# Attention and two MLPs on one core: three changes of order, and one operation of chunk 0 moved from VectorE to ScalarE

## The chip, the core and the metric

The kernel runs on one core of a Trainium2 chip. The metric is the device time of one execution in microseconds; the number to predict is the median over several executions of the changed kernel.

## What is computed

Four batches of 576 tokens go through an attention of eight heads of 64 (four heads look at the last 32 positions, four at every 32nd), then through two MLPs of 512 to 2048 to 512 features, all 2304 tokens. The weights come as float64.

```python
x = attention(q, k, v)                      # 2304 x 512
h = x @ w_in;   g = h * clip(h + 3, 0, 6) / 6;             x = g @ w_out
h = x @ w_in2;  g = maximum(h, 0) + log1p(exp(-abs(h)));   out = g @ w_out2
```

## The kernel before

Every large product is made of three matmuls, with each operand split into a high part (a rounding of 32 bits to the matmul's format) and a low part (the rest): high x high, high x low, low x high. ScalarE makes the high part with a copy, VectorE the low part with a subtraction. The float64 weights are loaded as raw 64-bit words; `w_scale` (L132, ScalarE) rescales the upper words and `w_bits` (L137 and L140, VectorE) puts three bits of the lower words under them, which gives float32 weights.

The **first MLP** is a row of 80 slots, 16 (one for each block f of 128 hidden features) for each of five chunks of tokens: chunk 0 of 384 tokens, the others of 480. `slot` (L1289) emits the hidden matmuls of its own f (`pe_h`, L776: psh from x and W_in), the activation (`post1`, `post2a`, `post2b`: L789, L790, L797, L803), and the output matmuls of the slot two before (`pe_y`, L820: psy from gh, gl and the halves woh, wol of W_out). Each is 12 matmuls. In chunk 0 a slot also makes the weights: `win_bits` and `win_split` for W_in, `wout_bits` and `wout_split` (L170 to L176) for W_out. Pieces of the attention for the next chunk are strewn between them from the table `fill`. From the eighth slot of chunk 1 on, two parts per slot of `prep` turn the weights of the second MLP into sums of blocks and their halves (L230, L248, L249), stored to the DRAM tiles sdr and sorted by a counter `k0` (L1293).

The **second MLP** uses Strassen's scheme, seven products in place of eight. Three chunks of 768 tokens (order `CHS`: 1, 2, 0) each have a first phase (`pe1`, L933, banks psm: 8 groups g of 7 units i) and a second one (`pe2`, L1077, banks psa and psn: 7 products of 8 units). A unit is six matmuls of 384 columns. `steps` (L1354) is the order of all units. A unit's weights su are loaded 10 units ahead on SP's queue (L908), and after each such load SP issues one waiting transfer of the list `dmas`: the stores of the output and the loads of the next chunk's x (`x_load`, xr from ydr), in the order in which `queue` (L883) took them. The loaded x pieces are summed on VectorE by `x_sums` (L859) in the same first phase. In that phase product 7 and then product 4 of a group add into one bank, and between them VectorE reads it (u, L915).

On each engine the instructions of a slot or unit keep the order in which they are written (`in_order`), so an instruction that waits holds all behind it. `do` (L1373) ties the casts and subtractions of the second phase's input (th, tl: L1008, L1012) to units.

Of the kernel before, what the change touches and what calls it, by code (L numbers as in the profile page):

```python
# [13 lines left out]
ALU = mybir.AluOpType  # L14
# [8 lines left out]
def attn_two_mlps(  # L23
# [21 lines left out]
    nc = tc.nc  # L45
# [6 lines left out]
    NF = DFF // P  # L52
# [15 lines left out]
    HT, NF2, DH = 384, NF // 2, DM // 2  # L68
# [55 lines left out]
    def words(o, l, f, dt):  # L124

        w = wst_t[o, l, f].bitcast(dt).rearrange("p (n t) -> p n t", t=2)
        return w[:, :, 0], w[:, :, 1]

    def w_scale(o, l, f):

        h = words(o, l, f, U32)[1].bitcast(F32)
        nc.scalar.activation(out=h, in_=h, func=AF.Prelu, scale=2.0**-112, alpha=-(2.0**32))  # L132

    def w_bits(o, l, f, out=None):
        low, _ = words(o, l, f, U32)
        m, e = words(o, l, f, I32)
        nc.vector.tensor_scalar(  # L137
            out=m, in0=low, scalar1=2.0**-29, scalar2=7.0, op0=ALU.mult, op1=ALU.min
        )
        nc.vector.scalar_tensor_tensor(  # L140
            out=e if out is None else out.bitcast(I32), in0=e, scalar=3, in1=m,
            op0=ALU.logical_shift_left, op1=ALU.bitwise_or,
        )
# [6 lines left out]
    def win_bits(f):  # L150
        wi_t[0, f] = sw_tile("wir", F32)
        w_bits(0, 0, f, wi_t[0, f])
        wst_t.pop((0, 0, f))
# [47 lines left out]
    def prep_load(o, g):  # L201
        for f in (2 * g, 2 * g + 1):
            (load_wout if o else load_win)(1, f)
# [633 lines left out]
    def half(c, t):  # L837

        return 2 * c + (t if c else 1 - t)

    def x_load(c, kl):
        raw = l2p["r" if kl and "r" in l2p else "x"].tile([P, 5, HT], F32, tag="xr", name="xr", bufs=1)
        xr_t[c, kl] = raw
        parts = []
        for slot, kt, t in ((0, kl, 0), (3, kl, 1), (1, kl + 2, 0), (2, kl + 2, 1)):
            a0 = a = half(c, t) * HT
            while a < a0 + HT:
                s = max(i for i in range(NC1) if Y0[i] <= a)
                z = min(a0 + HT, Y0[s + 1])
                parts.append((raw[:, slot, a - a0 : z - a0], ydr[s][kt, :, a - Y0[s] : z - Y0[s]]))  # L850
                a = z
        return parts
# [22 lines left out]
    pre, aft, dmas, now = {}, {}, [], [0]  # L875
# [4 lines left out]
    def after_post(d, fn, *a):  # L880
        aft.setdefault(now[0] + d, []).append(lambda: fn(*a))

    def queue(d, parts):  # L883
        dmas.extend((now[0] + d, o, i) for o, i in parts)

    @contextmanager
    def in_order():
# [105 lines left out]
    ORDER2 = (1, 5, 6, 2, 7, 4, 3)  # L993
# [134 lines left out]
    for b in range(B):  # L1128
        o = 2 * NF * b
# [33 lines left out]
    with ExitStack():  # L1163
# [5 lines left out]
        for i, t in enumerate(sq0):  # L1169
            nc.sync.dma_start(  # L1170
                out=t.rearrange("p (h i) d -> p h (i d)", h=2),
# [16 lines left out]
            out=mask, in_=mask, compare_op=ALU.is_ge, fill=NEG / SCALE, base=STRIDE,  # L1188
# [3 lines left out]
            out=ident, in_=ident, compare_op=ALU.not_equal, fill=1.0, base=0,  # L1192
# [3 lines left out]
            out=mask, in_=mask, compare_op=ALU.is_ge, fill=NEG / SCALE, base=-1,  # L1196
# [92 lines left out]
        def slot(n, l, c, f):  # L1289
            att = c < B  # L1290
            first_use = c == 0
            last1 = c == NC1 - 1
            k0 = 2 * n - 2 * NF - 14  # L1293

            if n == NF + 1:
                prep_load(0, 0)
            if last1 and f == 0:
                at.close()
                l2p["x"] = ctx.enter_context(tc.tile_pool(name="l2x", bufs=1, reuse_waits="tile"))
            pe_h(l, c, f)  # L1300
            if first_use:
                if f + 3 < NF:
                    w_scale(0, 0, f + 3)
                    win_bits(f + 3)
                if f + 2 < NF:
                    win_split(f + 2)
            post1(l, c, f)
            if not first_use:
                post2a(l, c, f)
            if att:  # L1310
                for u in fill.get(2 * n, []):
                    u()
            if first_use:
                w_scale(1, 0, f)
                wout_bits(f)
                post2a(l, c, f)
            post2b(l, c, f)
            if 0 < n <= NF:
                wout_split(n - 1)
            prep(k0)  # L1320
            if n >= 2:
                pe_y(*seq[n - 2])
            if att:
                for u in fill.get(2 * n + 1, []):
                    u()
            prep(k0 + 1)
            if first_use:
                load_first(2 * f + 11)
                load_first(2 * f + 12)
            if c == 1:  # L1330
                split_raw(c, f)
            if NF <= n + 3 < 2 * NF:
                load_raw(*seq[n + 3][1:])
            if 2 * NF <= n + 4 < len(seq):
                load_split(*seq[n + 4][1:])
            if last1 and f >= 1:
                kl, r = divmod(f - 1, 7)
                if r == 0 and kl < 2:
                    for o, i in x_load(CHS[0], kl):
                        nc.sync.dma_start(out=o, in_=i)  # L1340
                elif r == 3:
                    x_split(CHS[0], kl, 0)
                    x_sums(CHS[0], kl, False)
                elif r == 4:
                    x_sums(CHS[0], kl, True)
                    x_split(CHS[0], kl, 2)
                elif r == 5:
                    x_split(CHS[0], kl, 1)
# [5 lines left out]
        steps = []  # L1354
        for c in CHS:
            for g in range(NF2 + 1):
                for i in (1, -4, 6, -3, 2, 7, 5):
                    if (g < NF2) if i > 0 else (g > 0):
                        steps.append((c, 1, g - (i < 0), abs(i)))
            for i in ORDER2:  # L1360
                steps += [(c, 2, g, i) for g in range(NF2)]
        AHEAD = 10
        for k in range(AHEAD):
            s_unit(steps[k])
# [10 lines left out]

        for n, c in enumerate(CHS):
            nxt = CHS[n + 1] if n + 1 < NCH else None
            for k, gc, gs in ((3, 0, 1), (4, 1, 2), (5, 3, 4), (6, 4, 5), (7, 6, 7)):
                do(c, 1, gc, t_cast, c, k)
                do(c, 1, gs, t_sub, c, k)  # L1380
            for k in range(8, 4 * len(ORDER2)):
                p, q = divmod(k - 4, 4)
                do(c, ORDER2[p], 2 * q, t_cast, c, k)
                do(c, ORDER2[p], 2 * q + 1, t_sub, c, k)
            for i, g, j, q in (
                (5, 7, 7, 0), (6, 1, 7, 1), (6, 3, 7, 2), (2, 1, 7, 3),
                (2, 3, 4, 0), (2, 5, 4, 1), (7, 1, 4, 2), (7, 3, 4, 3),
            ):
                do(c, i, g, t_diff, c, j, q)
            if nxt is not None:  # L1390
                for i, g, kl, part in (
                    (5, 2, 0, 0), (5, 4, 1, 0), (3, 1, 0, 2), (3, 3, 1, 2), (3, 5, 0, 1), (3, 6, 1, 1)
                ):
                    do(c, i, g, x_split, nxt, kl, part)
                for kl in range(2):
                    do(c, 6, 5 + 2 * kl, x_sums, nxt, kl, True)
        for k, step in enumerate(steps):
            c, ph, g, i = step
            nxt = CHS[CHS.index(c) + 1] if c != CHS[-1] else None
            now[0] = k  # L1400
            with in_order():
                if k + AHEAD < len(steps):
                    s_unit(steps[k + AHEAD])
                for _ in range(1 if k + AHEAD < len(steps) else 2):
                    if dmas and dmas[0][0] <= k:
                        _, o, v = dmas.pop(0)
                        nc.sync.dma_start(out=o, in_=v)
                post = (pe1 if ph == 1 else pe2)(step)
                for u in pre.pop(k, []):
                    u()  # L1410
                early = ph == 1 and i == 3 and g in (2, 4, 6)
                if early:
                    t_cast(c, g // 2 - 1)
                if post:
                    post()
                if early:
                    t_sub(c, g // 2 - 1)
                for u in aft.pop(k, []):
                    u()
                if ph == 1:  # L1420
                    if nxt is not None and g in (1, 2) and i == 1:
                        queue(1, x_load(nxt, g - 1))
                    if nxt is not None and i == 2 and g in (4, 6):
                        x_sums(nxt, g // 2 - 2, False)
                else:
                    for u in at.get((c, i, g), []):
                        u()
# [70 lines left out]
```

## Time and profile before

| | us |
|---|---|
| three runs, median (lowest, highest) | 852.42 (848.24, 852.48) |
| profiled execution, its own time | 854.5 |
| its span | 852.6 |
| TensorE busy in it | 821.2 (96%) |
| VectorE busy | 636.0 (75%) |
| ScalarE busy | 456.9 (54%) |

In the profile, PE is TensorE's matmuls, PEld its weight loads, DVE VectorE, ACT ScalarE, POOL GpSimd, SP the engine that only issues transfers. A busy PE is the sum of modelled matmul intervals, which overlap; where it is busy throughout, the distance from start to start tells the pace. PEclk is the granted clock as a share of 2.4 GHz.

### The profile page before, as it was taken

The page shows a single profiled execution, that of the slowest core. Times are in us where ns is not written, and L with a number is a line of the kernel's source. Part 1 is how long each engine was busy: PE and PEld are TensorE (multiplying, and loading weights), DVE is VectorE, ACT ScalarE, POOL GpSimd, SP SyncE. Part 2 cuts the span into 40 slices and gives each one's busy share as a digit, 9 for nine tenths or more (in the row PEclk, how much of TensorE's full clock was granted, in tenths as well). Part 3 has the DMA queues.
Part 4 walks back from the last instruction along what each step waited for, and adds up shares of the span by engine and source line. Part 5 has one row for each costly group of instructions (what it writes and reads, how often), then busy time and mean ns, then how long its engine had stood idle before and what let it go on. Part 6 is the DMA issues. An engine that isn't in the chain of part 4 may idle for free.

```text
span 852.6 us, 16751 instructions
## 1 busy us (share of the span) xinstructions
PE 821.2 (96%) x6245; PEld 757.7 (89%) x6245; DVE 636.0 (75%) x1055; ACT 456.9 (54%) x754; POOL 88.5 (10%) x149
## 2 busy tenths in 40 slices
PE   5889999999999999999999999999998999999996
PEld 3779998888888888888888899999998999999996
DVE  5899966777776677866777568798667898587784
ACT  4567653455444444545555467854376834478530
POOL 3001122123211121111211200000000000000000
PEclk8899999999999999999999999999999999999998
DMA  9899777599969997796977798788899887997774
GB/s 308 227 281 328 160 232 269 143 342 343 373 206 244 302 334 281 217 302 201 328 269 259 247 359 258 243 250 245 259 281 311 247 246 220 303 306 245 247 248 114
DMA packets 169504, 225.42 MB, mean 264 GB/s; under 512 B 76432, under 2 KB 91664, under 8 KB 169424
## 3 DMA queue, kind: packets, MB, share of 16 engines
q1 hardware_dynamic: 154304, 176.71, 68.3%
q0 software_dynamic: 13312, 46.67, 14.5%
q10 hardware_dynamic: 1808, 0.98, 0.5%
q8 instruction: 50, 0.82, 0.4%
q14 instruction: 30, 0.25, 0.1%
HBM read 172.88 MB, written 51.38 MB: 263 GB/s over the span
## 4 chain that ended last, share of the span: by engine, by line
PE 56%; issue 17%; DVE 6%; ACT 4%; POOL 3%; DMA 3%; POOLq 0%; DVEq 0%; ACTq 0%; SPq 0%
PE psn L1077 15%; PE psm L933 13%; PE psy L820 10%; PE psh L776 10%; PE psa L1077 6%; POOL sdr L250 2%; DVE gq L915 2%; DVE gq L946 2%; DMA wo<-in_w_out_dram 1%; ACT r L952 1%; ACT r L981 1%; ACT r L951 1%; PE pso L717 1%; DMA xr<-ydr 1%; DVE u L915 1%
## 5 line engine op out<-in xcount | busy, mean ns | idle before, releaser
L933 PE MATMUL psm<-xh,su 128*128 128x384 f32 x672 | 173.4, 337 | 4.2 <-DVE u L915 4.2
L933 PEld LDWEIGHTS psm<-xh,su 128*128 128x128 f32 x672 | 122.5, 189 | 5.5 <-DVE u L915 5.5
L1077 PE MATMUL psn<-th,su 128*128 128x384 f32 x480 | 124.6, 339 | 0.0
L820 PE MATMUL psy<-gh,woh 128*128 128x480 f32 (+1 forms) x320 | 120.8, 381 | 2.7 <-ACT r L789 1.2
L820 PE MATMUL psy<-gh,wol 128*128 128x480 f32 (+1 forms) x320 | 120.2, 376 | 3.1 <-DVE wol L146 3.1
L776 PE MATMUL psh<-xh,wih 128*128 128x480 f32 (+1 forms) x320 | 120.3, 376 | 1.5 <-ACT xh L282 1.5
L820 PE MATMUL psy<-gl,woh 128*128 128x480 f32 (+1 forms) x320 | 119.2, 372 | 0.0
L776 PE MATMUL psh<-xl,wih 128*128 128x480 f32 (+1 forms) x320 | 118.6, 371 | 0.4 <-DVE xl L283 0.4
L776 PE MATMUL psh<-xh,wil 128*128 128x480 f32 (+1 forms) x320 | 118.8, 371 | 0.0
L933 PE MATMUL psm<-xl,su 128*128 128x384 f32 x336 | 112.9, 336 | 0.0
L1008 ACT CAST th<-gq 128x768 fp32r<-128x768 f32 x84 | 68.9, 834 | 69.7 <-PE psn L1077 43.0
L789 ACT ACTIVATE r<-psh 128x480 f32<-128x480 f32 (+1 forms) x80 | 44.6, 557 | 114.8 <-PE psh L776 112.1
L790 DVE SCALAR_TENSOR_TENSOR r<-r,psh 128x480 f32<-128x480 f32 (+1 forms) x80 | 50.4, 631 | 51.9 <-ACT r L789 51.9
L1077 PEld LDWEIGHTS psn<-th,su 128*128 128x128 f32 x480 | 87.5, 188 | 0.0
L797 ACT CAST gh<-r 128x480 fp32r<-128x480 f32 (+1 forms) x80 | 46.2, 578 | 75.9 <-DVE r L790 75.6
L1012 DVE TENSOR_TENSOR tl<-gq,th 128x768 fp32r<-128x768 f32 x84 | 77.7, 950 | 8.9 <-ACT th L1008 8.9
L1077 PE MATMUL psn<-tl,su 128*128 128x384 f32 x240 | 81.3, 339 | 0.0
L820 PEld LDWEIGHTS psy<-gh,wol 128*128 128x128 f32 x320 | 60.5, 189 | 12.6 <-DVE wol L146 4.4
L803 DVE TENSOR_TENSOR gl<-r,gh 128x480 fp32r<-128x480 f32 (+1 forms) x80 | 50.6, 633 | 26.2 <-ACT gh L797 26.0
L820 PEld LDWEIGHTS psy<-gh,woh 128*128 128x128 f32 x320 | 60.4, 189 | 10.5 <-ACT gh L797 1.4
L250 POOL DMA_DIRECT2D sdr<-so x64 | 43.7, 683 | 241.7 <-DVE so L249 208.6
L776 PEld LDWEIGHTS psh<-xh,wih 128*128 128x128 f32 x320 | 60.1, 188 | 9.6 <-ACT xh L282 2.0
(143 smaller groups left out, 1420.5 us busy)
## 6 DMA issues: line engine op xcount, KB each, us to landing
su<-sdr SPq DMA_DIRECT2D x336, 256.0 KB
sdr<-so POOLq DMA_DIRECT2D x48, 512.0 KB, 5.1
wi<-in_w_in_dram SPq DMA_DIRECT2D x32, 512.0 KB
wo<-in_w_out_dram SPq DMA_DIRECT2D x32, 512.0 KB
woh<-wdh SPq DMA_DIRECT2D x48, 256.0 KB
wol<-wdl SPq DMA_DIRECT2D x48, 256.0 KB
wdr<-wor POOLq DMA_DIRECT2D x16, 256.0 KB, 4.4
wol<-wdr SPq DMA_DIRECT2D x16, 256.0 KB
```

The costliest lines, as they stand in the source:

```text
L250: nc.gpsimd.dma_start(out=sdr[o][g][4 * i + a : 4 * i + z].rearrange("b p n -> p b n"), in_=t.rearrange("p b j n -> p b (j n)").bitcast(F32),)
L776: mark["PE"] = nc.tensor.matmul(ps[:, :n], lhsT=w[:, kt], rhs=x[:, :n], start=(kt == 0 and j == 0), stop=(kt == KT - 1 and j == 2),)
L789: nc.scalar.activation(out=r, in_=ps, func=AF.Relu, bias=3.0)
L790: mark["DVE"] = nc.vector.scalar_tensor_tensor(out=r, in0=r, scalar=6.0, in1=ps, op0=ALU.min, op1=ALU.mult)
L797: mark["ACT"] = nc.scalar.copy(hi, g32_t[l, c, f])
L803: nc.vector.tensor_tensor(out=lo, in0=g32_t.pop((l, c, f)), in1=hi.bitcast(F32), op=ALU.subtract)
L820: mark["PE"] = nc.tensor.matmul(psy_t[l, c][m][:, :w], lhsT=a, rhs=bb, start=(f == 0 and j == 0), stop=(f == NF - 1 and j == 2),)
L915: return nc.vector.tensor_tensor(out=out_, in0=x, in1=y, op=op)
L933: nc.tensor.matmul(ps, lhsT=w[:, kl], rhs=x, start=i in (1, 5, 6) and kl == 0 and j == 0, stop=kl == 1 and j == 2, skip_group_check=True,)
L1008: nc.scalar.copy(tt[c, k][0], t_raw(c, k))
L1012: nc.vector.tensor_tensor(out=lo, in0=t_raw(c, k), in1=hi.bitcast(F32), op=ALU.subtract)
L1077: nc.tensor.matmul(psl[mt][:, :HT], lhsT=w[:, mt], rhs=x, start=i in (1, 4, 5, 6) and gg == 0 and j == 0, stop=gg == NF2 - 1 and j == 2, s ...
```

## The change

Four edits. In chunk 0's `wout_bits` the low words of W_out are turned into the three bits by a multiplication on ScalarE that rounds into integers, in place of VectorE's multiply and min. `queue` can put its parts at the head of the list, and the x loads use that. `k0` is two larger, so that all of `prep` comes one slot earlier. In `steps` the first two units of the second phase stand one ahead of the first phase's last unit 4 and one ahead of its last unit 3; the cast and subtraction numbers 3 and 4 are tied one unit later in the table, since the units that they name now come earlier.

```diff
@@ w_bits
-        nc.vector.tensor_scalar(
-            out=m, in0=low, scalar1=2.0**-29, scalar2=7.0, op0=ALU.mult, op1=ALU.min
-        )
+        if o and not l:
+            nc.scalar.mul(m, low, 7.4999 * 2.0**-32)
+        else:
+            nc.vector.tensor_scalar(
+                out=m, in0=low, scalar1=2.0**-29, scalar2=7.0, op0=ALU.mult, op1=ALU.min
+            )
@@
-    def queue(d, parts):
-        dmas.extend((now[0] + d, o, i) for o, i in parts)
+    def queue(d, parts, first=False):
+        n = 0 if first else len(dmas)
+        dmas[n:n] = [(now[0] + d, o, i) for o, i in parts]
@@ slot
-            k0 = 2 * n - 2 * NF - 14
+            k0 = 2 * n - 2 * NF - 12
@@ steps
-            for i in ORDER2:
-                steps += [(c, 2, g, i) for g in range(NF2)]
+            last = [steps.pop(), steps.pop()]
+            two = [(c, 2, g, i) for i in ORDER2 for g in range(NF2)]
+            steps += [two[0], last[1], two[1], last[0]] + two[2:]
@@
-            for k, gc, gs in ((3, 0, 1), (4, 1, 2), (5, 3, 4), (6, 4, 5), (7, 6, 7)):
+            for k, gc, gs in ((3, 1, 2), (4, 2, 3), (5, 3, 4), (6, 4, 5), (7, 6, 7)):
@@
-                        queue(1, x_load(nxt, g - 1))
+                        queue(0, x_load(nxt, g - 1), True)
```

**What moves on the engines.** ScalarE in slot 2 of chunk 0 (wo_442 are the raw words of that slot's block of W_out, wi_444 those of a later block of W_in), before:

```order
L132 ACTIVATE wi_432<-wi_432 128x512
L160 CAST wih<-wir 128x512
L789 ACTIVATE r<-psh 128x384
L132 ACTIVATE wo_442<-wo_442 128x512
L797 CAST gh<-r 128x384
L175 CAST woh<-wor 128x512
L681 ACTIVATE sc_94<-sc_94 128x8x64
```

and now:

```order
L163 CAST wih<-wir 128x512
L792 ACTIVATE r<-psh 128x384
L132 ACTIVATE wo_442<-wo_442 128x512
L138 ACTIVATE wo_442<-wo_442 128x512
L800 CAST gh<-r 128x384
L178 CAST woh<-wor 128x512
L684 ACTIVATE sc_94<-sc_94 128x8x64
```

L138 is the new operation; gh and woh come behind it, and VectorE's L143 (L140 before) now needs it.

SP in the first phase of the second chunk (ot are output tiles on their way to DRAM, su weights, xr the x pieces of the next chunk), before, from row 445 of its program:

```order
L1407 DMA out_0_dram<-ot_7034 32x3x128
L908 DMA su_7506<-sdr0_5_153 128x512
L1407 DMA out_0_dram<-ot_7034 32x3x128
L908 DMA su_7515<-sdr0_4_152 128x512
L1407 DMA xr_7285<-ydr1_96 128x384
L908 DMA su_7526<-sdr0_5_153 128x512
L1407 DMA xr_7285<-ydr0_95 128x384
```

and now, from row 411:

```order
L1412 DMA out_0_dram<-ot_6945 32x3x128
L912 DMA su_7286<-sdr0_2_150 128x512
L1412 DMA xr_7285<-ydr1_96 128x384
L912 DMA su_7296<-sdr0_2_150 128x512
L1412 DMA xr_7285<-ydr0_95 128x384
```

The first four x pieces stand 36 rows earlier, which is 18 loads of su; the other four stand at row 427 in place of 457, 15 loads earlier; 8 stores go behind them.

TensorE where the first phase ends (psm_6500 is the bank of products 6, 7 and 4 of group 7, psm_6549 that of 5 and 3, psa those of the second phase), before:

```order
L933 MATMUL psm_6549<-xl1_5679,su_6426 128x384
L933 MATMUL psm_6549<-xh1_5678,su_6426 128x384
L933 MATMUL psm_6500<-xh0_5349,su_6441 128x384
L933 MATMUL psm_6500<-xl0_5350,su_6441 128x384
L933 MATMUL psm_6500<-xh0_5349,su_6441 128x384
```

and now:

```order
L937 MATMUL psm_6549<-xl1_5686,su_6426 128x384
L937 MATMUL psm_6549<-xh1_5685,su_6426 128x384
L1081 MATMUL psa_6562<-th_6182,su_6441 128x384
L1081 MATMUL psa_6562<-tl_6183,su_6441 128x384
L1081 MATMUL psa_6562<-th_6182,su_6441 128x384
L1081 MATMUL psa_6563<-th_6182,su_6441 128x384
L1081 MATMUL psa_6563<-tl_6183,su_6441 128x384
L1081 MATMUL psa_6563<-th_6182,su_6441 128x384
L937 MATMUL psm_6500<-xh0_5356,su_6451 128x384
```

A unit of the second phase now lies between the last unit 5 and the last unit 4; another lies between the units 4 and 3.

## Rows read from the trace of the kernel before

**Rows 1.** Page, part 1: busy time, share of the span and instructions of each engine.

```profile
PE 821.2 (96%) x6245; PEld 757.7 (89%) x6245; DVE 636.0 (75%) x1055; ACT 456.9 (54%) x754; POOL 88.5 (10%) x149
```

**Rows 2.** Windows: stretch, length, busy (count) PE PEld DVE ACT POOL, PEclk, DMA, GB/s.

```profile
36.00:46.20 10.20, 7.75 (x45) 6.46 (x38) 9.85 (x19) 6.18 (x13) 0.91 (x2) 1.00 1.04 214
...
46.20:49.60 3.40, 2.92 (x9) 2.93 (x10) 3.26 (x6) 1.57 (x3) 0.18 (x1) 0.51 0.94 365
...
114.10:478.50 364.40, 363.23 (x3170) 312.50 (x3169) 257.60 (x445) 175.60 (x296) 68.96 (x111) 1.00 0.83 272
...
643.50:646.90 3.40, 3.40 (x12) 3.40 (x12) 3.22 (x5) 2.35 (x4) 0.00 (x0) 0.50 1.07 392
...
646.90:845.00 198.10, 197.38 (x1123) 196.38 (x1121) 154.71 (x220) 110.86 (x154) 0.00 (x0) 1.00 0.80 247
```

**Rows 3.** Waits of PE, whole span: who waited for whom, total us, times, longest.

```profile
PE psm L933 <- DVE u L915: 4.2, 4, 2.9
...
PE psy L820 <- DVE wol L146: 3.1, 4, 1.8
...
PE pso L717 <- issue: 1.9, 1, 1.9
...
PE psy L820 <- ACT r L789: 1.2, 1, 1.2
...
PE psy L820 <- ACT gh L797: 1.0, 1, 1.0
...
PE psy L820 <- ACT woh L175: 0.6, 2, 0.3
```

**Rows 4.** Groups by line, 36 to 114 us: count, busy us, mean ns, idle before.

```profile
L132 ACT ACTIVATE wo<-wo 128x512 f32<-128x512 f32 x15 | 10.4, 691 | 0.0
...
L797 ACT CAST gh<-r 128x384 fp32r<-128x384 f32 x15 | 7.7, 514 | 10.8 <-DVE r L790 10.6
...
L789 ACT ACTIVATE r<-psh 128x384 f32<-128x384 f32 x14 | 6.9, 491 | 13.5 <-PE psh L776 13.0 <-PE psq L614 0.5
...
L137 DVE TENSOR_SCALAR wo<-wo 128x512 int32<-128x512 uint32 x15 | 6.3, 418 | 0.0
```

**Rows 5.** Timeline of DVE, slots 0 and 2: start us, length us, work [idle before].

```profile
34.09 0.69 DVE L140 SCALAR_TENSOR_TENSOR wor<-wo 128x512 int32<-128x512 int32 x1
...
44.33 0.42 DVE L137 TENSOR_SCALAR wo<-wo 128x512 int32<-128x512 uint32 x1
...
44.85 0.69 DVE L140 SCALAR_TENSOR_TENSOR wor<-wo 128x512 int32<-128x512 int32 x1
...
45.93 0.69 DVE L146 TENSOR_TENSOR wol<-wor,woh 128x512 fp32r<-128x512 f32 x1
```

**Rows 6.** Timeline of ACT, slot 0.

```profile
32.96 0.67 ACT L132 ACTIVATE wo<-wo 128x512 f32<-128x512 f32 x1
```

**Rows 7.** Timeline of all engines, 638 to 642 us.

```profile
638.39 0.56 DVE L859 TENSOR_TENSOR xr<-xr 128x384 f32<-128x384 f32 x1 [1.93 <-DMA xr<-ydr]
...
638.73 0.34 PE L933 MATMUL psm<-xh,su 128*128 128x384 f32 x1
...
640.94 0.56 DVE L859 TENSOR_TENSOR xr<-xr 128x384 f32<-128x384 f32 x1 [1.99 <-DMA xr<-ydr]
...
642.01 0.44 PE L933 MATMUL psm<-xh,su 128*128 128x384 f32 x1 [2.94 <-DVE u L915]
```

**Rows 8.** Timeline of PE, end of the first phase of the first chunk.

```profile
541.06 0.34 PE L933 MATMUL psm<-xh,su 128*128 128x384 f32 x1
541.95 0.44 PE L933 MATMUL psm<-xh,su 128*128 128x384 f32 x1 [0.55 <-DVE u L915]
```

**Rows 9.** Timeline of ACT, last two slots of the first MLP.

```profile
477.55 2.42 ACT L248 CAST so<-wo 128x512 fp32r<-128x512 f32 x2
479.77 0.61 ACT L789 ACTIVATE r<-psh 128x480 f32<-128x480 f32 x1
```

**Rows 10.** DMA queues, 57.9 to 59.3 us: packets, MB, share of 16 engines.

```profile
q8 instruction: 1, 0.02, 4.6%
```

## The prediction, made before the changed kernel ran

> **What bounds the kernel now.** I read the page first: TensorE is busy for 821.2 of 852.6 us [rows 1], so at most some 31 us are to be had, and whatever does not shorten or fill an idle stretch of TensorE is worth nothing. The stretches come next [rows 2]: from 114.1 to 478.5 us TensorE is busy for 363.23 of 364.40 us, from 646.9 to 845 us for 197.38 of 198.10 us. A matmul of 384 columns costs 198.10 / 1123 = 0.176 us there. Between lie two stretches of 3.40 us with a granted clock of 0.51 and 0.50, that is 1.2 GHz instead of 2.4; each costs half its length, 1.7 us. Third I read who TensorE waits for [rows 3]: 4.2 us for VectorE's reads of a psm bank (one wait of 2.9, three small ones), 3.1 + 0.6 us for the halves of W_out, 1.0 us for a gh, and 1.9 and 1.2 us for nothing that the row explains (the first says "issue"; the second names a ScalarE instruction that does not feed it). What is left is startup before 36 us and the tail after 845 us, which the change does not touch.
>
> **The change, part by part.**
>
> *x loads ahead of stores.* At 638.39 and 640.94 VectorE stands still for 1.9 us each before the two sums of L859, because the x pieces have not landed [rows 7]; behind them in its queue lies the L915 that frees the psm bank for the matmul of 642.01. From the matmul of 638.73 to that one pass 3.28 us instead of 0.18, so 3.1 us are lost; and then the clock falls to 0.50 for 3.40 us [rows 2], another 1.7. The SP rows put the first four x pieces 18 places, and the next four 15 places, earlier; SP issues one of these a unit, and a unit of six matmuls takes 6 x 0.176 = 1.06 us, so the pieces come 16 to 19 us sooner, where the two waits ask for 4. The wait goes whole, and with it the cause of the low clock: **-4.8 us**. The output stores come eight places later; their tile is next written by the second phase of the following chunk, dozens of units on, so nobody waits. Cover gone would mean the weights: the same queue brings 256 KB a unit, ten units ahead, and eight x pieces of 192 KB more are 1.5 MB in the way, some 4 us at the 392 GB/s that the queues reach [rows 2]; the lead is 10.6 us. Bounds: 0 to -4.8, and I take the upper one.
>
> *Two units moved.* At the end of the first phase the last unit 4 of g = 7 adds into a bank that VectorE still reads; the matmul of 541.95 starts 0.89 us after the one before it instead of 0.18 [rows 8], a loss of 0.71 with 0.55 of it counted as idle. There are three such places, one in each chunk: 4.2 - 2.9 = 1.3 us idle [rows 3] plus 0.16 each for the pipeline, 1.8 us. Now a unit of the second phase stands ahead of it (1.06 us of work that needs a long finished cast), more than each wait. **-1.8 us**; bounds 0 to -1.8. What comes in return: the cast for k = 3 moves no later on TensorE's clock, and its subtraction one unit, with four units still to go before its matmul.
>
> *Sums sooner.* The preparation of the second MLP's weights ends a slot earlier. ScalarE's last relu of the first MLP starts only at 479.77, behind 2.42 us of casts of that preparation [rows 9], and TensorE waits 1.0 us for the gh made from it [rows 3]. With nothing in ScalarE's last two slots that wait goes: **-1.0 us**; bounds 0 to -1.2. The same work meets the attention pieces one slot earlier over 55 slots; TensorE loses 1.2 us in 364 there today [rows 2], so other meetings may cost as much again: +1.2 at most goes into the range.
>
> *Low words on ScalarE in chunk 0.* VectorE loses 16 instructions of 418 ns [rows 4], each of which holds it for 0.52 us (44.33 to 44.85) [rows 5]. ScalarE gains 16 that the trace does not show: one input, 512 elements at stride two, unsigned integer in, integer out. Nearest is its own L132 on the same tile, 691 ns, below it the cast of 384 dense elements, 514 ns [rows 4]; what integer ends cost no row says, so I keep twice L132, 1.4 us, as the upper end and take 0.69. Is there room? In 36 to 114 us ScalarE idles 10.8 + 13.5 = 24.3 us before L797 and L789 [rows 4], 15 x 0.69 is 10.4. Yes, and even 15 x 1.4 = 21 fits.
> First the row, then the rule: VectorE does this in 418 ns and ScalarE needs 691 for the like [rows 4]. The Trainium skill says against this edit that multiplications belong on VectorE and not on ScalarE (ScalarE: Activation LUTs, Rules for kernel authors), and its formula for immediates gives an estimate of 0.61 us. On price the trace agrees; the rule's outcome, ScalarE as the new bound, is the third rival below.
> What does VectorE's gain reach? It is busy for 9.85 of the 10.20 us from 36 to 46.2 [rows 2], slots 2 and 3, and the bound there; later TensorE is. The wait that ends at the wol of 45.93 [rows 5] has three of the moved instructions ahead of it. The first gives nothing: ScalarE's L132 starts at 32.96 [rows 6] and its second one would end near 34.2, while VectorE starts L140 at 34.09 already [rows 5]. The other two give 0.5 each: -1.0. The wait shrinks from about 2.4 us to 1.4; I keep the low clock after it (0.51 in 46.2 to 49.6 [rows 2]). The waits for wol in slots 11 and 15, the rest of the 3.1 + 0.6 us, have a dozen moved instructions ahead and go, with their pipeline refill 1.0 us. **-2.0 us**. Bounds: 0, if ScalarE merely takes VectorE's place, and -5.4 with all 3.7 us and the low clock gone.
>
> **Sum.** 4.8 + 1.8 + 1.0 + 2.0 = 9.6 us. The profiled execution took 854.5 us (852.6 of span and 1.9 around it), so 844.9; it lies 2.1 above the median of the three runs, 852.42. From the median: **842.8 us**. A measurement can tell 0.5% from no change, 4.3 us here.
>
> **Rivals.**
> *More than the sum (0.13).* The shorter wait in slot 3 no longer drops the clock (-1.7), and the bare waits of 1.9 and 1.2 us go as well. For: a packet on the instruction queue lies just ahead of the first [rows 10], so it is a matter of when, not of dependence. Against: TensorE's own program is unchanged there. 842.8 - 4.8 = 838.0 us. The Trainium skill (Runtime: NRT & Kernel Launch, Instruction fetch mechanics) calls such fetches mostly hidden; a bare wait behind one would be an exception.
> *Only the second MLP gains (0.17).* The ScalarE operation delays wor and gh as much as VectorE is relieved, or new meetings eat the rest: -4.8 - 1.8 - 1.0 = 844.8 us.
> *ScalarE becomes the bound of chunk 0 (0.05), slower than before.* Each operation needs 24.3 / 15 = 1.6 us before ScalarE's idle time is used up; from there on each 0.1 us costs 1.5 us. At 2.6 us, nearly four times L132, it is 15 x 1.0 = 15 us lost against 7.6 gained: 852.4 + 7.4 = 859.8 us. For: no row shows integers on this engine. Against: the factor needed.
> *The x pieces starve the weights (0.07).* If the 4 us of x traffic delay the su loads beyond their lead, TensorE waits in units 1 to 12 of that phase instead, and the low clock may come back there: the 4.8 us return, 847.6 us. For: the DMA share is 1.07 just after the place where the pieces are read today [rows 2]. Against: the first chunk issues its x pieces in the same place with no wait of TensorE in [rows 3].
>
> **How the numbers follow.** Forecast 0.58, more 0.13, second MLP only 0.17, starving 0.07, slower 0.05. The range runs from 837.5 (just under the case of more) to 847.5 (starving, or the chunk 0 and meeting bounds together: 842.8 + 2.0 + 1.2 = 846.0, and the runs of before themselves spread 4.2 us). Faster by over 4.3 us means below 848.1: all cases but the slower one, less half of the starving one: 0.88. Same: 0.08. Slower: 0.04.
>
> **What would show it.** Right: no wait before L859; no stretch of clock 0.50 between 600 and 660 us; TensorE's waits on L915 near 0; the last relu of the first MLP right after its matmuls; the new ScalarE group near 0.69 us; and in chunk 0 the waits for wol down from 3.1 to about 1.5 us. Wrong: a new ScalarE group of over 1.6 us, idle time of VectorE before L143 for ScalarE, TensorE waiting for su, or new waits of TensorE between 150 and 480 us.

## The result, and the profile after

The changed kernel takes 841.66 us (median of 6 runs, 840.85 to 844.41), the kernel before beside it 850.36 us (median of 6, 848.24 to 852.48): ratio 0.9904, 95% interval 0.9879 to 0.9928, so 6.1 to 10.3 us less. Measured a second time (after_again below) it was 842.61 against 850.87 us, ratio 0.9904 again (0.9889 to 0.9918). The forecast was 842.8 us, 837.5 to 847.5.

The profiled execution of the changed kernel took 841.76 us, near its median; that of before took 854.5, 4.1 us above its median. The two profiles therefore differ by 12.7 us, more than the kernels do, and a part of what follows is about that difference.

First the page of the changed kernel, part 1:

```profile
PE 815.2 (97%) x6245; PEld 755.1 (90%) x6245; DVE 628.8 (75%) x1039; ACT 464.4 (55%) x770; POOL 88.6 (11%) x149
```

TensorE has the same 6245 matmuls [rows 1]. VectorE has 16 instructions fewer and ScalarE 16 more, 7 us each way. Next the waits of PE over the whole span (who waited for whom, total us, times, longest):

```profile
PE psy L823 <- DVE wol L149: 1.8, 2, 1.3
...
PE pso L720 <- issue: 1.1, 1, 1.1
PE pss L644 <- issue: 0.7, 1, 0.7
```

Against [rows 3] the 4.2 us for the psm bank, the 1.0 us for gh and the 1.2 us put down to r are gone from the list; wol went from 3.1 to 1.8. The windows of the changed kernel, with the columns of [rows 2]:

```profile
36.00:46.20 10.20, 8.88 (x116) 8.15 (x107) 10.03 (x18) 7.84 (x15) 1.09 (x2) 1.00 1.17 247
110.80:475.00 364.20, 364.20 (x3174) 313.41 (x3174) 261.25 (x450) 178.09 (x300) 70.45 (x113) 1.00 0.84 276
592.00:660.00 68.00, 68.00 (x393) 68.00 (x392) 51.41 (x85) 44.22 (x67) 0.00 (x0) 1.00 0.93 305
660.00:832.00 172.00, 172.00 (x981) 171.83 (x980) 134.95 (x187) 92.76 (x128) 0.00 (x0) 1.00 0.80 247
```

In none of the last three windows has TensorE an idle stretch left, and the stretch of half clock near 640 us is gone: the granted clock is 1.00, that is 2.4 GHz, throughout 592 to 660. What remains to be had lies before 110 us and in the tail. The groups by line, 36 to 111 us (count, busy us, mean ns, idle of the engine before them and for whom):

```profile
L143 DVE SCALAR_TENSOR_TENSOR wor<-wo 128x512 int32<-128x512 int32 x15 | 10.2, 681 | 3.6 <-ACT wo L138 3.6
L138 ACT ACTIVATE wo<-wo 128x512 int32<-128x512 uint32 x15 | 10.0, 666 | 0.0
...
L800 ACT CAST gh<-r 128x384 fp32r<-128x384 f32 x15 | 7.6, 509 | 3.4 <-DVE r L793 3.3
L792 ACT ACTIVATE r<-psh 128x384 f32<-128x384 f32 x14 | 6.9, 492 | 11.8 <-PE psh L779 11.3 <-PE psq L617 0.4
```

The new operation takes 666 ns (0.69 was forecast). ScalarE's idle time before L800 and L792 fell from 24.3 [rows 4] to 15.2 us. VectorE now waits 3.6 us for the new operation, which the forecast listed as a sign of failure; none of it falls between 36 and 60 us, where TensorE still waits for wol, and behind that TensorE waits for no wol or woh.

### The profile page after: what moved, and what is told of

Its sections match the earlier page's. It is cut to its first block, busy times and chain, and to the rows that moved or that the text cites. A ratio compares the mean times of both kernels' runs of the same rounds, so it can differ in the third digit from the quotient of the medians.

```text
span 840.0 us, 16748 instructions
## 1 busy us (share of the span) xinstructions
PE 815.2 (97%) x6245; PEld 755.1 (90%) x6245; DVE 628.8 (75%) x1039; ACT 464.4 (55%) x770; POOL 88.6 (11%) x149
## 4 chain that ended last, share of the span: by engine, by line
PE 94%; DVE 2%; DMA 1%; ACT 1%; issue 1%; DVEq 0%
PE psy L823 24%; PE psh L779 23%; PE psm L937 21%; PE psn L1081 15%; PE psa L1081 6%; PE pso L720 1%; PE pss L644 1%; PE psx L746 1%; PE psp L700 1%; DMA wi<-in_w_in_dram 1%; DMA lq<-in_ql_dram 1%; PE psd L412 0%; ACT s L373 0%; ACT sc L373 0%; PE pst L503 0%
## 5 line engine op out<-in xcount | busy, mean ns | idle before, releaser
L792 ACT ACTIVATE r<-psh 128x480 f32<-128x480 f32 (+1 forms) x80 | 44.6, 557 | 103.0 <-PE psh L779 102.4
L793 DVE SCALAR_TENSOR_TENSOR r<-r,psh 128x480 f32<-128x480 f32 (+1 forms) x80 | 50.5, 631 | 47.5 <-ACT r L792 47.3
L800 ACT CAST gh<-r 128x480 fp32r<-128x480 f32 (+1 forms) x80 | 46.2, 577 | 68.8 <-DVE r L793 68.7
L779 PEld LDWEIGHTS psh<-xl,wih 128*128 128x128 f32 x320 | 60.5, 189 | 8.3 <-DVE xl L286 0.9
```

Source lines behind the costliest of these rows:

```text
L779: mark["PE"] = nc.tensor.matmul(ps[:, :n], lhsT=w[:, kt], rhs=x[:, :n], start=(kt == 0 and j == 0), stop=(kt == KT - 1 and j == 2),)
L792: nc.scalar.activation(out=r, in_=ps, func=AF.Relu, bias=3.0)
L793: mark["DVE"] = nc.vector.scalar_tensor_tensor(out=r, in0=r, scalar=6.0, in1=ps, op0=ALU.min, op1=ALU.mult)
L800: mark["ACT"] = nc.scalar.copy(hi, g32_t[l, c, f])
```

## The experiments

Eleven more runs followed, one of them the kernel before and one the changed kernel once again. To compare their profiles, the start times of the matmuls were used to cut each span into four: up to the first matmul of the first MLP, chunk 0 (its 16 slots), the rest of the first MLP, and the second MLP with the tail. "x", "u", "k", "a" mark the edits that a kernel holds: x loads first, units moved, k0, ScalarE's operation.

| kernel | edits | start | chunk 0 | rest of first MLP | second MLP |
|---|---|---|---|---|---|
| before | none | 27.50 | 86.66 | 370.88 | 367.52 |
| before_again | none | 26.55 | 89.36 | 369.35 | 365.60 |
| x_first | x | 27.30 | 87.58 | 369.61 | 363.36 |
| two_units | u | 26.97 | 86.50 | 369.77 | 362.43 |
| sums_sooner | k | 28.07 | 87.03 | 368.31 | 365.96 |
| act_bits | a | 27.30 | 83.49 | 370.37 | 365.35 |
| no_x | u k a | 27.93 | 83.74 | 368.34 | 363.18 |
| changed kernel | x u k a | 26.45 | 84.35 | 368.38 | 360.80 |
| after_again | x u k a | 27.18 | 83.31 | 368.40 | 361.08 |
| late_win | x u k a and more | 26.68 | 83.98 | 368.48 | 361.17 |
| act_win | x u k a and more | 29.84 | 83.59 | 368.08 | 360.57 |
| act_win_slots | x u k a and more | 27.08 | 87.22 | 368.68 | 360.95 |
| act_twice | x u k a and more | 28.68 | 86.70 | 368.34 | 360.98 |

The two profiles of the unchanged kernel differ by 2.7, 1.5 and 1.9 us in the last three columns. Each edit shows in the column of its stage, and in the other columns nothing stands out from that spread.

### Each edit alone

**x_first**: in the kernel before, only the `queue(..., first=True)` edit, which also drops its delay of one unit (the diff is cut to the call).

```diff
-                        queue(1, x_load(nxt, g - 1))
+                        queue(0, x_load(nxt, g - 1), True)
```

> The kernel before with one edit alone: the x loads go to the head of the list. Theory (the forecast's first term): VectorE no longer waits for the x pieces, TensorE's start-to-start gap of 3.28 us near 638 us goes, and no stretch of granted clock 0.50 stands between 600 and 660 us; 4.8 us less than the kernel before (3.1 of wait, 1.7 of clock). Rival (the x pieces starve the weights): TensorE waits for su in the same phase instead, and the gain is 0 to 2 us. Second rival: the wait goes but the low clock stays somewhere in the second MLP, 3.1 us.

Measured: ratio 0.9978 (0.9961 to 0.9995), 1.9 us less, 0.4 to 3.3. The wait of VectorE is gone: both sums run in one piece, with no idle time before them (timeline of DVE, x_first: start, length, work):

```profile
635.85 1.15 DVE L859 TENSOR_TENSOR xr<-xr 128x384 f32<-128x384 f32 x2
```

No low clock stands near 640 us, and TensorE waits for no su. The psm line of its waits has only the three short ones at the ends of the phases left:

```profile
PE psm L934 <- DVE u L916: 1.7, 3, 0.6
```

So the mechanism is the forecast's, but the gain is 0.4 of its size. Further runs (below) show why.

**two_units**: only the order of the two units, with the cast and subtraction numbers that belong to it (not in the cut shown).

```diff
-            for i in ORDER2:
-                steps += [(c, 2, g, i) for g in range(NF2)]
+            last = [steps.pop(), steps.pop()]
+            two = [(c, 2, g, i) for i in ORDER2 for g in range(NF2)]
+            steps += [two[0], last[1], two[1], last[0]] + two[2:]
```

> The kernel before with one edit alone: two units of the second phase stand ahead of the first phase's last two, with the cast and subtraction numbers that go with it. Theory: the three small gaps of TensorE behind VectorE's read of a psm bank (0.3 to 0.7 us over a matmul's pace) go: 1.8 us less at most. Of these the one near 638 us cannot be told from the wait for the x pieces, which stays; so the profile should show the gaps at the first and third chunk's phase end gone and the gap of 638 us at 3 us. Rival: the waits come back one unit later, since the bank is read by the same VectorE instructions: 0.

Measured: ratio 0.9967 (0.9941 to 0.9993), 2.8 us less, 0.6 to 5.0. The psm line of PE's waits in this run has one wait left, the one for the x pieces:

```profile
PE psm L933 <- DVE u L915: 1.3, 1, 1.3
```

The three at the ends of the phases are gone. In the changed kernel the place of [rows 8] reads (timeline of PE):

```profile
535.19 0.33 PE L937 MATMUL psm<-xh,su 128*128 128x384 f32 x1
535.36 0.34 PE L1081 MATMUL psa<-th,su 128*128 128x384 f32 x1
...
536.42 0.34 PE L937 MATMUL psm<-xh,su 128*128 128x384 f32 x1
```

The unit of the second phase fills 1.06 us at a matmul's pace, and the bank is free behind it. In the five profiles with the old order the three losses (start to start, over a matmul's 0.18) sum to 1.75, 2.33, 2.16, 2.34 and 2.57 us, mean 2.2; the first profile, on which the 1.8 rested, had the smallest. The expectation was wrong in one detail: the wait near 638 us is not one of the three. The phase ends are at 541, 664 and 782 us in the profile of before.

**sums_sooner**: only `k0`.

```diff
-            k0 = 2 * n - 2 * NF - 14
+            k0 = 2 * n - 2 * NF - 12
```

> The kernel before with one edit alone: the preparation of the second MLP's weights comes one slot earlier. Theory: the last relu of the first MLP starts right behind its matmuls and TensorE's start-to-start gap of 1.15 us near 481 us goes; nothing else moves: 1.0 us less, which no timing of five rounds may tell from none; the profile must show the gap gone. Rival: the earlier preparation meets the attention pieces worse, and new waits between 120 and 470 us of 1 us or more eat it: 0 or up to 1.2 us more. The one wait of 1.3 us near 243 us, which the changed kernel no longer has, is also watched: if it is gone here, this edit removed it.

Measured: ratio 0.9976 (0.9955 to 0.9998), 2.0 us less, 0.2 to 3.8. Both gaps are gone, the one near 481 and the one near 243 us, and no new one stands between. ScalarE at the end of the first MLP, in the changed kernel (timeline of ACT):

```profile
471.57 0.57 ACT L792 ACTIVATE r<-psh 128x480 f32<-128x480 f32 x1 [0.73 <-PE psh L779]
472.86 0.59 ACT L800 CAST gh<-r 128x480 fp32r<-128x480 f32 x1 [0.72 <-DVE r L793]
```

The relu now waits for its matmuls, where [rows 9] had it behind 2.42 us of casts. In the five profiles without this edit the two gaps are together 2.5, 0.9, 1.2, 1.4 and 2.0 us, mean 1.6; the means of the table's third stage, 370.0 without and 368.4 with the edit, differ by 1.6 as well.

**act_bits**: only ScalarE's operation (the diff is cut to its first lines).

```diff
+        if o and not l:
+            nc.scalar.mul(m, low, 7.4999 * 2.0**-32)
+        else:
```

> The kernel before with one edit alone: in chunk 0 ScalarE turns the low words of W_out into three bits. Theory (the forecast's fourth term): 2.0 us less, all before 115 us; slots 11 and 15 without a wait for wol; the wait in slot 3 or 4 about 1.4 us in place of 2.4. Rival: VectorE is relieved but its next instruction waits for ScalarE as long, 0 us. Rival on the clock: with the shorter wait no stretch of clock 0.5 stands between 36 and 60 us, 1.7 us more, 3.7 us less than before in all. The ScalarE group should read 0.67 us, as in the changed kernel.

Measured: ratio 0.9955 (0.9939 to 0.9971), 3.8 us less, 2.5 to 5.2; the operation takes 672 ns. Chunk 0 has a mean of 87.4 us in the five profiles without it and 83.7 in the four that have it and no further edit: 3.7. (Without before_again, which has three stretches of half clock between 30 and 65 us where the other four have one, it is 86.9, and the gain 3.2.) The waits for wol in slots 11 and 15 are gone, and the one of slot 3 is 0.53 us shorter (1.48 against 2.01 us over a matmul's pace). The rival on the clock fell: half clock for 3.41 us stands at 46.5 us here as at 46.2 before. The waits of PE for wol, and then those at the two places where [rows 3] has it wait for nothing that the row explains (the bare waits, near 243 and near 59 us):

```profile
PE psy L823 <- DVE wol L149: 1.3, 1, 1.3
...
PE psy L823 <- ACT r L792: 0.9, 1, 0.9
PE pso L720 <- issue: 0.8, 1, 0.8
```

The last was 1.9 in [rows 3]; the forecast's sum did not count it, and a part of the gain may lie there (below).

### What the wait for the x pieces costs

**before_again**: the kernel before, unchanged, in one more profile.

> The kernel before, unchanged, profiled a second time. Theory (the wait for the x pieces varies from one execution to the next, and the first profile had a long one): TensorE's loss near 638 us is 1 to 2.5 us, with no low clock behind it between 600 and 660 us. Rival (3.1 us and a low clock are the rule for the kernel before, and the single edits of other places changed it): 3.0 us or more again, with the low clock. The bare wait near 59 us: in nine executions a wait for nothing that the profile shows ended 1.4 to 1.6 us after the end of a packet of the instruction queue; here too, if that is its cause.

Measured: 852.88 us. The same place as [rows 7], timelines of DVE and PE:

```profile
639.18 0.56 DVE L859 TENSOR_TENSOR xr<-xr 128x384 f32<-128x384 f32 x1 [2.03 <-DMA xr<-ydr]
```

```profile
638.96 0.34 PE L933 MATMUL psm<-xh,su 128*128 128x384 f32 x1
640.26 0.44 PE L933 MATMUL psm<-xh,su 128*128 128x384 f32 x1 [0.97 <-DVE u L915]
```

One of the two sums waits here, not both, and TensorE loses 1.1 us instead of 3.1. The window behind it has the full clock:

```profile
644.00:660.00 16.00, 16.00 (x95) 16.00 (x94) 13.74 (x24) 11.47 (x18) 0.00 (x0) 1.00 0.88 302
```

**no_x**: the changed kernel, with the x loads at the end of the list again (the diff of x_first, undone).

> The changed kernel with one edit undone: the x loads go to the end of the list again. Theory: the wait for the x pieces comes back; in four executions with that order it cost 3.1, 2.4, 1.5 and 1.0 us of TensorE's time, and only the longest was followed by a low clock. So 1 to 2.5 us more than the changed kernel, and no stretch of clock 0.50 near 640 us unless the wait is 3 us or longer. Rival (the forecast's price): 4.8 us more, with the low clock.

Measured: 844.24 us, ratio to before 0.9917 (0.9905 to 0.9928), against 0.9904 of after_again beside it: 1.6 us more by the medians. By timing alone that is not clear of no difference (the two intervals overlap); in the profile the wait is back with 1.4 us from start to start, without a low clock:

```profile
PE psm L936 <- DVE u L918: 1.3, 1, 1.3
```

Six profiles with the stores first now show this loss: 3.1, 1.1, 2.4, 1.5, 1.0 and 1.4 us, mean 1.8, and half clock behind it in the first alone (1.7 / 6 = 0.3 on average). That makes about 2 us, in agreement with the 1.9 of x_first and the 1.6 of no_x. The wait and its cause were read rightly; the price was that of the worst execution seen. That the long wait brought on the low clock rests on that one execution.

### Do the edits add?

**after_again**: the changed kernel once more.

> The changed kernel itself once more, beside the next three on one chip. The four edits alone were worth 1.9, 2.8, 2.0 and 3.8 us, 10.5 together. Theory (they add, since each takes a wait in a place of its own): 10 to 11 us less than the kernel before, ratio near 0.988. Rival (they overlap): 8 us or less, ratio 0.990 or above.

Measured: ratio 0.9904 (0.9889 to 0.9918), 8.3 us less. By the letter of the expectation that is the rival's side. But the four single gains add to 10.5 us with about 3.5 to either side (their half intervals, 1.5, 2.2, 1.8 and 1.4 us, added as squares; more, since all four are measured against the same runs of before), so timing does not tell the two apart. The mean stages do add: 3.7 in chunk 0, 1.6 behind it, 5.2 in the second MLP (366.1 in the four profiles with neither x nor u, 360.9 in the two with all four edits), 10.5 in all, from profiles of which the two of the kernel before lie 4.1 and 2.8 us above its medians. For the second MLP the traces settle it: up to its last matmul it takes 352.7 us in both profiles of the changed kernel, the seven others above it in the table take 1.5 to 7.0 us more, and in each of them its gaps between matmuls, with what half clock cost, give that surplus to 0.2 us. So x and u do not take from each other there. In chunk 0, with its spread, an overlap of 1 or 2 us stays possible.

### ScalarE's room in chunk 0

**act_twice**: the changed kernel with a second operation on ScalarE, which changes no value.

```diff
             nc.scalar.mul(m, low, 7.4999 * 2.0**-32)
+            nc.scalar.mul(m, m, 1.0)
```

> The changed kernel with the new ScalarE operation issued twice (the second one multiplies its result by 1). ScalarE then spends 1.33 us per slot on it. Theory (the forecast's third rival: ScalarE has 1.6 us per slot to spare before it is the bound): at most 1 to 2 us more than the changed kernel, from slots 0 to 3, where VectorE waits for it already. Rival (what counts is not ScalarE's idle time but that wor, woh, wol and gh come later in each slot): the gain of this edit, 3.8 us, is gone or more.

Measured: 844.62 us, 2.0 more than after_again (0.2 to 3.6 by the spread of the runs); 0.9923 (0.9909 to 0.9938). So about half of the edit's gain is gone, at 1.35 us per slot on ScalarE where the forecast had set the point of loss at 1.6. Chunk 0 took 86.70 us, 3.4 more than in after_again's profile and 2.4 more than in the first one of the changed kernel. The waits of PE:

```profile
PE psy L824 <- DVE wol L150: 2.3, 4, 1.3
PE psy L824 <- ACT woh L179: 1.5, 2, 1.2
...
PE pso L721 <- issue: 1.4, 1, 1.4
```

and ScalarE and VectorE in slot 2, where that new wait of 1.2 us for woh lies (timelines):

```profile
39.59 0.69 ACT L138 ACTIVATE wo<-wo 128x512 int32<-128x512 uint32 x1
40.30 0.66 ACT L139 ACTIVATE wo<-wo 128x512 int32<-128x512 int32 x1
40.86 0.50 ACT L801 CAST gh<-r 128x384 fp32r<-128x384 f32 x1
41.27 0.61 ACT L179 CAST woh<-wor 128x512 fp32r<-128x512 f32 x1
```

```profile
41.00 0.69 DVE L144 SCALAR_TENSOR_TENSOR wor<-wo 128x512 int32<-128x512 int32 x1 [0.37 <-ACT wo L139]
41.61 0.55 DVE L807 TENSOR_TENSOR gl<-r,gh 128x384 fp32r<-128x384 f32 x1
```

ScalarE works in the order written, so the cast to woh stands behind the second multiplication and ends at 41.88; TensorE starts at 41.93. ScalarE's idle time is not used up: 6.4 us of it are left before L801 and L793 from 36 to 111 us. In this slot it is the place of the operation, ahead of what TensorE needs, which counts. Of the 3.4 us against after_again this wait makes 0.9 and the bare wait near 60 us, which no run ties to ScalarE, another 1.0; the rest are waits for wol and woh in slot 2, at 54 and at 113 us. The size of the loss is the theory's (1 to 2 us), its mechanism the rival's; the whole 3.8 us, which the rival forecast, did not go.

**act_win** and **act_win_slots**: the changed kernel, with the low words of W_in on ScalarE too; in the second run only for the blocks made within the slots (the diff is that of the first).

```diff
-        if o and not l:
+        if not l:
```

> The changed kernel with the low words of W_in, too, turned into bits by ScalarE (16 more operations of 0.67 us, 16 fewer of 0.42 us on VectorE). Theory (VectorE is still the bound of slots 2 and 3: TensorE waits 1.5 and 0.6 us for wol there): the waits shrink by two to three times 0.4 us, 0.5 to 1 us less than the changed kernel. Rival (ScalarE now holds the chain wi, wih and the relu of each slot): new waits of TensorE for gh or wih in chunk 0, 1 to 5 us more than the changed kernel.

> The changed kernel with the low words of W_in, too, on ScalarE, but only for the 13 blocks whose bits are made in the slots, not for the three made before the first slot. Theory (the run with all 16 lost 1.3 us in timing and showed the first matmul of the first MLP 1.2 to 3.4 us later and chunk 0 itself no longer than the changed kernel's, 83.6 against 83.3 and 84.4 us): the loss was the startup, so this is level with the changed kernel, ratio to before 0.989 to 0.991. Rival (ScalarE's further load costs in the slots): 1 us or more over the changed kernel.

Measured: 843.88 us, 0.9914 (0.9898 to 0.9930), and 844.92 us, 0.9932 (0.9910 to 0.9954): neither is better than the changed kernel. In act_win chunk 0 was as long as the changed kernel's, and the start later (29.84 us). act_win_slots misses the range that its theory gave: its start is normal, and its chunk 0 took 87.22 us, 3.9 more than in after_again. But its profile does not put that on ScalarE's load in the slots. TensorE's matmuls of chunk 0 come in the same order in all these kernels, so their distances can be compared one by one: the bare wait is 2.6 us longer, half clock (10.2 us of it in chunk 0, 3.4 in after_again) costs some 2.6 us more, and the waits for wol and woh are 1.4 us shorter. What the further operations cost thus stays open. Why they bring nothing is easier to see: VectorE no longer has these instructions, but it idles for ScalarE before both of L143's kinds, wor and wir (act_win_slots, the bare wait and then groups by line, 36 to 111 us):

```profile
PE pso L720 <- issue: 3.0, 1, 3.0
```

```profile
L143 DVE SCALAR_TENSOR_TENSOR wor<-wo 128x512 int32<-128x512 int32 x15 | 10.3, 688 | 4.2 <-ACT wo L138 3.9 <-DMA wi<-in_w_in_dram 0.4
...
L143 DVE SCALAR_TENSOR_TENSOR wir<-wi 128x512 int32<-128x512 int32 x12 | 8.3, 688 | 3.4 <-ACT wi L138 3.4
```

**late_win**: the changed kernel with W_in's halves made behind W_out's in each slot.

```diff
-                if f + 2 < NF:
-                    win_split(f + 2)
@@
                 wout_split(n - 1)
+            if first_use and f + 2 < NF:
+                win_split(f + 2)
```

> The changed kernel with one more move: in chunk 0 the halves of a later block of W_in are made at the end of a slot, behind the halves of W_out, in place of ahead of the activation. Theory (in slots 2 to 4 VectorE works without a pause and TensorE waits 1.5 us in one and 0.6 us in another for a wol that has a wil of 0.6 us ahead of it): those waits shrink to 0.9 and 0, so 1.0 to 1.5 us less than the changed kernel. Rival (the wil and wih are then late for their own slot, or the pieces of the attention are): TensorE waits for wil or wih instead, 0 or slower.

Measured: 841.74 us, 0.9895 (0.9871 to 0.9918); level with the changed kernel. The wait in slot 3 kept its size (1.3 us idle, 1.48 over a matmul's pace, as in the changed kernel), though the wil of that slot left its place (timeline of DVE, late_win, from wol to wol):

```profile
37.85 0.69 DVE L149 TENSOR_TENSOR wol<-wor,woh 128x512 fp32r<-128x512 f32 x1
38.46 0.69 DVE L149 TENSOR_TENSOR wil<-wir,wih 128x512 fp32r<-128x512 f32 x1
39.06 1.28 DVE L668 TENSOR_TENSOR sc<-pss,bmask 128x512 f32<-128x512 f32 x2
...
41.86 0.68 DVE L677 TENSOR_REDUCE nm<-sc 128x8 f32<-128x512 f32 x1
42.57 0.69 DVE L678 TENSOR_TENSOR sc<-sc,nm 128x512 f32<-128x512 f32 x1
...
44.25 0.69 DVE L149 TENSOR_TENSOR wol<-wor,woh 128x512 fp32r<-128x512 f32 x1
```

From one wol to the next pass 6.4 us, in which VectorE never stops: its work there is the same whichever way it is ordered, since one wil lies between two wol in either order. TensorE waited for the first of them too, so the second wait is VectorE's work of the slot less TensorE's. That would also explain why ScalarE's edit shortened this wait by just one instruction (0.53 us) and not by all that had been taken away up to there. Of the 6.4 us the attention's pieces (L668, L677, L678) are 2.6; strewing these over other slots is what might shorten it. That was not tried.

## Why the prediction was right, and where its terms were not

The median and the range held, in part by luck, through terms whose errors cancelled. Measured alone, the four edits are worth 10.5 us where 9.6 were summed: the first term was 2.9 too large, the other three together 3.8 too small. The base was off as well: 852.42, the median of three runs, lies 2.1 above that of the six, 850.36, from which the same sum gives 840.8 us. All four waits that the forecast named went or shrank for the reason given, but a part of the gain lies at two bare waits that its sum left out. (The chance of being faster, 0.88, does not follow from the cases listed for it: they add to 0.92.)

- *x loads ahead of stores*, -4.8 forecast: -1.9 measured alone (0.4 to 3.3), 1.6 undone. The step that was mis-sized is "3.1 us are lost; and then the clock falls to 0.50 for 3.40 us [rows 2], another 1.7", taken whole from one profile. The loss averages 1.8 us over six profiles, and the low clock followed once in six. The cover named for it held: no wait for su appeared, and the pieces starve nothing.
- *Two units moved*, -1.8: -2.8 measured (0.6 to 5.0), 2.2 by the gaps of five profiles. Right, its size again that of one profile, here a small one.
- *Sums sooner*, -1.0: -2.0 measured (0.2 to 3.8), 1.6 by the gaps. The drain wait went as described (its mean is 0.7 us). What was missing is the bare wait near 243 us, 1.2 in [rows 3], which the forecast named only in the rival of more; this edit removes it too (all five profiles without the edit have it, none of the eight with it). No new meetings of 1 us came.
- *Low words on ScalarE*, -2.0: -3.8 measured (2.5 to 5.2). The price of the operation was right (0.666 us for 0.69), slots 11 and 15 gave their 1.0 us, slots 2 and 3 gave 0.3 and 0.5 for the 1.0 summed. Over all profiles the term itself comes out: the lines for wol and woh in PE's waits sum to 3.9 us on average in the five without the edit and to 1.8 in the four with it, 2.1 less. Not in the sum was the bare wait near 59 us: a loss of 2.0, 2.6, 3.0, 1.2 and 1.4 us in the five profiles without the edit (mean 2.0), and 1.3, 0.6, 1.0 and 0.6 in the four with it (mean 0.9). That would be 1.1 us of the missing 1.8. But that the edit shortens this wait is not shown: with still more work on ScalarE in each slot it is 2.6, 3.1 and 1.6 us (act_win, act_win_slots, act_twice).
- Of the rivals, *more than the sum* had half of it right: the bare wait near 243 us went, and the one near 59 us is 1.3 and 0.6 us in the changed kernel's two profiles, though the first of them has one of 0.9 us near 79 us besides. Its other half, no low clock in chunk 0, did not come: 3.41 us of it stand at 31.1 and at 46.2 us in the two profiles of the changed kernel. *ScalarE becomes the bound* was rightly thought unlikely, but its threshold was wrong: act_twice loses 2.0 us at 1.35 us an operation, since the 1.6 was worked out from ScalarE's idle total and not from what stands behind the operation in one slot. The Trainium skill's rule against multiplications on ScalarE (ScalarE: Activation LUTs, Rules for kernel authors) holds here on price, 0.67 against 0.42 us. It did not hold as advice: the edit against it gained 3.8 us, since the cheaper engine was the one that TensorE waited for.

## What to carry to other kernels

One profile gives the cause of a wait, not its price: a wait for a DMA here lost 1.0 to 3.1 us from execution to execution, so profile the unchanged kernel two or three times before summing, above all when the profiled execution is slower than the median. A wait that one slot passes on to the next is sized by the whole work, in a cycle, of the engine that is waited for: in slot 3 here, moving an instruction off that engine helped by its length, and reordering within the cycle did not. When moving work to an idle engine, look at what stands behind it in that engine's queue, not at the idle total.

## What was not expected of the hardware

The bare waits are tied to the instruction queue. The times below are each from the trace: TensorE's last start before the wait, the end of the last packet of the instruction queue, and TensorE's next start.

```
kernel         last start  packet ends  next start  next - packet
before            58.67       59.25        60.74        1.49
before_again      58.40       59.41        61.01        1.60
x_first           58.44       59.96        61.49        1.52
two_units         58.83       58.56        60.06        1.50
sums_sooner       60.12       60.11        61.58        1.48
act_bits          57.43       56.92        58.48        1.56
no_x              58.75       57.77        59.35        1.58
changed kernel    56.27       56.10        57.62        1.52
changed kernel    78.72       77.99        79.61        1.62
after_again       57.29       56.30        57.92        1.61
late_win          56.78       56.24        57.69        1.45
late_win          78.77       77.90        79.39        1.50
act_win           57.18       58.37        59.80        1.42
act_win_slots     57.24       58.87        60.42        1.55
act_twice         60.46       60.67        62.09        1.42
before           243.47      243.77       245.02        1.25
before_again     245.28      244.60       245.90        1.30
x_first          244.19      243.82       245.09        1.28
two_units        242.80      242.54       243.80        1.26
act_bits         240.07      239.91       241.36        1.45
```

Wherever such a wait is, TensorE goes on 1.25 to 1.62 us after a packet has ended, however long it has stood by then (0.6 to 3.2 us from start to start). The wait is longer the later the packet comes. The profile names it as "issue", or, near 243 us in two profiles, as a wait for an instruction of ScalarE (in before it had ended 0.5 us earlier). The one near 57 us in the changed kernel:

```profile
57.62 0.29 PE L720 MATMUL pso<-vl,pt 64*32 64x64 f32 x8 [1.14 <-issue]
```

The Trainium skill calls instruction fetches mostly hidden (Runtime: NRT & Kernel Launch, Instruction fetch mechanics); in this kernel one or two of the 50 packets of a span were not.

Place and count in the traces say the same as the distance. The waits near 59 us come when TensorE has started 961 instructions (matmuls, weight loads and the semaphore instructions on record) in all 13 kernels, those near 79 us at 1473, those near 243 us at 4801. The packet ahead of them is always the 3rd, the 5th and the 18th of the 50 packets of 16 KB: 256 instructions to a packet. Counted on like this to every packet of the 13 profiles, the distance from a packet's end to the first instruction behind its seam is nowhere under 1.25 us. At the 18th packet it is 1.25 to 1.45 us in the five kernels without the edit of `k0`, where TensorE stands, and 2.0 to 2.2 in the eight with it, where it does not. So TensorE stood at a seam of its program until the packet had come, though no run moved a packet alone. What sets the moment at which a packet is fetched, and why the 18th came earlier, against TensorE's own progress, with the edit of `k0`, stays open.
